# Dummy products of a recurrent-attention and maxout kernel in float32 instead of half precision, with new orders of work

## The chip, the cores and the metric

The kernel runs on one core of one Trainium2 chip. The metric is the device time in microseconds (us). In the profile PE is TensorE, DVE is VectorE, ACT is ScalarE, POOL is GpSimd and SP is SyncE, which here only issues loads. Stores are issued from ACT.

## The reference

The first part is a gated linear recurrence over 768 steps for 4 x 8 heads of width 48. Its output, as 3072 rows of 384, goes through a maxout layer with two weight matrices of 384 x 1024 and an output matrix of 1024 x 384. All data are float32.

```python
for t in range(S):
    state = alpha[:, :, t, :, None] * state + np.einsum('bhd,bhe->bhde', k[:, :, t], v[:, :, t])
    y[:, :, t] = np.einsum('bhd,bhde->bhe', q[:, :, t], state)
...
h1 = x @ w1
h2 = x @ w2
g = np.maximum(h1, h2)
return (g @ w_out).astype(np.float32)
```

## The kernel before, in words

The work is cut into 12 units of 256 time steps of one batch (u = 0 to 11), each of two chunks of 128 steps; units 0 and 1 are cut in two halves of four heads more. For a unit u the kernel loads alpha, k, q and v (`ld.af`, `ld.kf`, `ld.qf`, `ld.vf`, L345), takes the logarithm of alpha on ACT (`lg`), adds pairs of steps (`sg`, DVE or POOL, L459), and sums along time with a triangular matrix on PE (`cs`, L479 and L481). Exponentials of these sums (`em`, `ep`, `de` on ACT) scale k and q (`kn`, `qn`). PE transposes both (`tpk`, `tpq`, L507), multiplies them (`pp`, L533), and DVE masks the products (`pt`, L550 for the halves, L545 for whole units). `kv` (L582) makes a chunk's contribution to the state, `tm` and `sb` carry the state on, and `y` (L642) gives the recurrence's output, which `xt` takes to SBUF.

The maxout uses max(h1, h2) = h2 + relu(h1 - h2): `w12` is w1 - w2, the `h` steps (L672) multiply by it, `g` applies the relu (L677, L678), and the `o` steps (L699) multiply by w_out and add x times (w2 w_out). That last matrix is made in the kernel's head: w2 is transposed on PE in float32 (`wt`, L382), copied (`wtc`), and multiplied by w_out in half precision (`wq`, L404).

The order of everything is written by hand, or rather found by a search outside the kernel: `ORDERS` lists for PE, ACT, DVE, POOL and SP the steps in the order in which each engine runs them, and by being in an engine's list a step is also assigned to it. `Plan.follow` walks these lists with a duration for each step and a set of rules and gives every step a planned start and a PSUM bank. Among the rules is one for PE's instructions: it counts them (`ni` for each step, two for each product: a weight load and the product) and supposes that a new block of instructions must have arrived after 189 and then after every 256.

Where the plan shows PE without work for more than 0.25 us in the first 45 us, `gaps` and `fill` put dummy products on a scratch tile of zeros, `wsrc` (L819; the tile is cleared at L825 by the first DVE instruction, ahead of everything). A gap is filled up to 0.25 us before the planned start of the next step. In the gap that starts at the very beginning a product is reckoned at double time (`slow`). The dummies stand in PE's instruction stream between the real steps, and PE runs its stream in order. `Plan.fills` says how many dummies the plan counts for a gap.

Of the kernel before, what the change touches and what calls it, by code (L numbers as in the profile page):

```python
# [201 lines left out]
cs4 h2.3 h2.0 h2.2 pp3 cs5 h2.1 o2.1.x0 o2.0.x0 o2.0.f0 o2.1.f0 tpq4 tpk4 y3 o2.1.f1 o2.0.f1 o2.0.f2 o2.1.f2
o2.0.f3 pp4 o2.1.f3 h3.3 h3.1 h3.0 o3.0.x0 kv4 tpq5 tpk5 kv5 cs6 h3.2 o3.0.f0 o3.0.f1 o3.1.x0 y4 o3.1.f0 o3.1.f1
o3.0.f2 o3.1.f2 o3.1.f3 pp5 h4.2 cs7 h4.1 o3.0.f3 h4.0 tpk6 kv6 tpq6 y5 o4.0.x0 o4.1.x0 o4.1.f0 h4.3 h5.0
o4.0.f0 h5.1 o4.1.f1 o4.0.f1 o4.1.f2 o4.1.f3 tpq7 tpk7 pp6 o4.0.f2 o5.1.x0 cs8 o4.0.f3 h5.2 h5.3 o5.1.f0 o5.1.f1
y6 kv7 tpk8 tpq8 o5.1.f2 o5.0.x0 o5.1.f3 o5.0.f0 o5.0.f1 pp7 o5.0.f2 cs9 h6.3 o5.0.f3 h6.0 h6.2 y7 pp8 tpk9 tpq9
# [10 lines left out]
de1.0 qk0.0.0 ep0.1 qk0.0.1 vc1 w1.00 w0.11 qk1.0.0 qk1.1.0 qk1.1.1 woc.0 wtc.20 qk0.1.1 w0.01 w0.10 wtc.21
w1.10 wtc.10 wtc.00 woc.2 xt1.0 woc.3 wtc.01 woc.4 xt0.1 woc.5 g0.0 lg2 woc.6 g1.1 lg3 ra2 de2 em2 wqc.0 wqc.2
ep2 g1.2 ra3 g0.3 wqc.1 de3 em3 ep3 qk2.0 oc0.1 w2.01 w2.10 w2.11 oc1.1 vc3 oc0.0 lg4 lg5 xt2.0 ra4 oc1.0 em4
w3.00 ep4 de4 g2.0 g2.2 w3.11 w3.10 de5 ra5 lg6 em5 ep5 ra6 xt3.1 xt3.0 vc4 w4.01 oc2.0 vc5 oc2.1 g3.3 g3.1 g3.0  # L220
w4.00 st0 w5.01 qk5.0 de6 w4.10 em6 g3.2 ep6 lg7 xt4.0 xt4.1 lg8 oc3.1 g4.2 em7 g4.1 oc3.0 st1 ra7 w7.10 de7
w6.01 w6.00 xt5.1 xt5.0 ep7 lg9 g4.3 g5.0 ra8 g5.1 oc4.1 w6.11 qk7.0 em8 de8 st2 ep8 g5.2 g5.3 lg10 oc4.0 xt6.1
qk8.0 ra9 oc5.1 xt6.0 em9 g6.3 ep9 oc5.0 de9 g6.0 g6.2 w9.10 st3 xt7.0 vc8 qk9.1 g6.1 st4 g7.3 lg11 st5 vc10
g7.0 w9.11 ra10 em11 de11 ep11 w10.01 ra11 w10.11 em10 xt8.0 xt8.1 de10 ep10 oc7.0 xt9.1 g8.1 w11.00 xt9.0
w10.00 g8.2 st6 w11.11 st7 qk10.0 qk11.0 g9.0 g9.1 g9.2 g9.3 xt10.0 xt11.0 g11.2 st9 g10.2 oc8.0 g10.3 oc8.1 st8
oc10.0 oc10.1 st10 st11.0 oc11.1 st11.1 st11.2
# [3 lines left out]
q00.0 qn0.0 kn1.1 q01.1 dm0 q01.0 k01.0 k00.1 qn1.1 qn1.0 qn0.1 pt0.0.1 qk1.0.1 pt0.0.0 tm1.0 pt1.0.0 qk0.1.0  # L230
tm0.0 pt1.1.1 pt1.1.0 pt1.0.1 pt0.1.1 pt0.1.0 tm0.1 xt1.1 zw2 xt0.0 w12.0 tm1.1 w12.1 wtc.11 g1.0 w12.2 g0.2
g0.1 w12.3 sg3 q02 qn2 k02 kn2 dm3 g1.3 qk2.1 qn3 k03 w2.00 tm2.0 pt2.0 pt2.1 tm3.0 qk3.1 xt2.1 qk3.0 tm3.1 g2.3
tm2.1 qn4 pt3.1 pt3.0 g2.1 qk4.0 qk4.1 k05 sg6 pt4.0 qn5 pt4.1 tm4.0 qk5.1 tm5.0 tm4.1 sb5.1 w5.00 k06 tm5.1 qn6
sg7 dm6 pt5.0 pt5.1 tm6.0 g4.0 dm7 vc7 k07 qk6.0 qk6.1 qn7 sb6.1 w7.11 tm6.1 qk7.1 pt6.1 pt6.0 qn8 kn8 w7.01
tm7.0 qk8.1 k09 pt7.1 pt7.0 tm7.1 qn9 xt7.1 dm9 pt8.1 pt8.0 qk9.0 g7.2 g7.1 sg11 tm8.0 tm9.0 sb9.1 pt9.0 pt9.1
q011 k010 oc6.1 oc6.0 q010 w9.01 kn10 k011 w11.01 qn10 qn11 oc7.1 sb11.0 g8.0 tm11.0 qk11.1 g8.3 qk10.1 tm10.0
w11.10 pt10.0 pt10.1 sb10.1 w10.10 pt11.0 pt11.1 xt10.1 oc9.0 g10.0 xt11.1 g10.1 g11.1 oc9.1 g11.0 g11.3 oc11.0
oc11.2
# [509 lines left out]
def kernel(  # L748
# [63 lines left out]
    def fill(t0, t1, b):  # L812

        left = t1 - t0 - 0.25
        w = env["wsrc"]
        slow = 2.0 if t0 < 1.5 else 1.0
        while left > 0.06:
            cols = min(512, int(2400 * left / slow) - 5)
            nc.tensor.matmul(env["PB"][b][:, 0:cols], lhsT=w[:, 0:128], rhs=w[:, 0:cols], start=True, stop=True)  # L819
# [38 lines left out]
```

## Time and profile before

| | |
|---|---|
| median of three runs | 133.82 us (133.79 to 133.96) |
| the profiled execution's own time | 133.79 us |
| its span, first to last instruction | 132.1 us |
| PE busy | 124.8 us, 2061 products |
| DVE / ACT / POOL busy | 103.3 / 95.4 / 64.4 us |
| dummy products (L819) | 28, first at 1.3, last at 12.5 us |
| HBM read / written | 23.59 / 4.72 MB |

The rows of the timeline give a start and a length in us, the engine, the line, what is written and what is read, and how many instructions are merged; in brackets stands how long the engine was idle before and what ended that. PE's products overlap in a pipeline, so that the length of a row is longer than the distance to the next one. The rows by stage give for each stretch its length, then the busy time of PE, of PE's weight loads, of DVE, ACT and POOL, each with a count, then PE's granted clock, the share of the transfer engines and GB/s.

### The profile page before, as it was taken

The page shows a single profiled execution, that of the slowest core. Times are in us where ns is not written, and L with a number is a line of the kernel's source. Part 1 is how long each engine was busy: PE and PEld are TensorE (multiplying, and loading weights), DVE is VectorE, ACT ScalarE, POOL GpSimd, SP SyncE. Part 2 cuts the span into 40 slices and gives each one's busy share as a digit, 9 for nine tenths or more (in the row PEclk, how much of TensorE's full clock was granted, in tenths as well). Part 3 has the DMA queues.
Part 4 walks back from the last instruction along what each step waited for, and adds up shares of the span by engine and source line. Part 5 has one row for each costly group of instructions (what it writes and reads, how often), then busy time and mean ns, then how long its engine had stood idle before and what let it go on. Part 6 is the DMA issues. An engine that isn't in the chain of part 4 may idle for free.

```text
span 132.1 us, 4911 instructions
## 1 busy us (share of the span) xinstructions
PE 124.8 (95%) x2061; PEld 88.9 (67%) x2061; DVE 103.3 (78%) x186; ACT 95.4 (72%) x198; POOL 64.4 (49%) x104
## 2 busy tenths in 40 slices
PE   6988889999999999999999999999999999999970
PEld 2444667777667766867776767976688765778650
DVE  5469997869999996998699969989988599355040
ACT  3688889568899999998996997998288920301540
POOL 6025970052759999958579399655146200000000
PEclk9999999999999999999999999999999999999999
DMA  3999999999999999999999999560003300002144
GB/s 89 325 325 363 415 371 342 341 297 260 252 302 311 280 261 293 322 334 251 318 314 270 300 275 285 193 241 5 0 5 122 121 0 0 5 0 90 69 181 144
DMA packets 56486, 28.63 MB, mean 217 GB/s; under 512 B 50320, under 2 KB 56080, under 8 KB 56464
## 3 DMA queue, kind: packets, MB, share of 16 engines
...
q10 hardware_dynamic: 3424, 4.72, 9.9%
q8 instruction: 16, 0.26, 0.7%
q14 instruction: 6, 0.05, 0.1%
HBM read 23.59 MB, written 4.72 MB: 214 GB/s over the span
## 4 chain that ended last, share of the span: by engine, by line
PE 68%; SPq 7%; DVE 7%; DMA 6%; issue 4%; POOL 4%; DVEq 0%; POOLq 0%
PE pb L699 28%; PE pb L672 20%; PE pb L642 7%; SPq L345 6%; DMA w2f<-in_moe_w_dram 6%; PE pb L533 4%; PE pb L582 3%; PE pb L507 3%; PE pb L404 2%; SPq L367 2%; POOL kn L414 1%; DVE gt L677 1%; PE pb L382 1%; PE pb L479 1%; DVE w L417 1%
## 5 line engine op out<-in xcount | busy, mean ns | idle before, releaser
L699 PE MATMUL pb<-wo,gt 128*128 128x384 f16 (+2 forms) x200 | 37.5, 320 | 0.0
L672 PE MATMUL pb<-xt,w 128*128 128x256 f16 x288 | 36.5, 273 | 0.0
L672 PEld LDWEIGHTS <-w 128*128 128x128 f16 x288 | 27.6, 98 | 5.7
L678 ACT ACTIVATE gt<-pb 128x512 f16<-128x512 f32 x32 | 18.4, 600 | 11.5 <-PE pb L672 11.0
L545 DVE TENSOR_TENSOR pt<-pb,mask 128x1024 f16<-128x1024 f32 x20 | 23.6, 1217 | 2.5 <-PE pb L533 2.5
L699 PEld LDWEIGHTS <-gt 128*128 128x128 f16 x200 | 18.2, 98 | 9.9
L677 DVE TENSOR_SCALAR gt<-pb 128x512 f16<-128x512 f32 x16 | 10.9, 685 | 9.2 <-PE pb L672 8.8
L699 PE MATMUL pb<-w2o,xt 128*128 128x384 f16 (+2 forms) x75 | 15.2, 320 | 0.0
L417 ACT CAST xt<-pb 128x384 f16<-128x384 f32 x18 | 10.1, 592 | 5.6 <-PE pb L642 5.6
L414 POOL TENSOR_TENSOR sb<-tm,dd 128x384 f16<-128x384 f32 x15 | 12.9, 858 | 1.2 <-DVE tm L614 1.0
L614 DVE TENSOR_TENSOR tm<-pb,sb 128x384 f32<-128x384 f32 x16 | 8.6, 550 | 3.8 <-PE pb L582 3.5
L417 ACT COPY qk<-pb 128x1024 f16<-128x1024 f16 (+1 forms) x13 | 10.3, 818 | 1.6 <-PE pb L507 1.4
L417 ACT COPY os<-pb 128x384 f32<-128x384 f32 (+1 forms) x18 | 8.5, 473 | 3.9 <-PE pb L699 2.8
L819 PE MATMUL pb<-wsrc 128*128 128x512 f16 (+6 forms) x28 | 9.4, 480 | 1.3 <-DVE wsrc L825 1.3
L642 PE MATMUL pb<-pt,w 128*32 128x128 f16 x384 | 10.0, 220 | 0.0
L414 POOL TENSOR_TENSOR kn<-kf,em 128x768 f16<-128x768 f32 (+1 forms) x5 | 7.5, 1498 | 5.0 <-DVE kf L414 3.3
L417 DVE COPY qk<-pb 128x1024 f16<-128x1024 f16 (+1 forms) x15 | 9.5, 646 | 0.3
L414 POOL TENSOR_TENSOR qf<-qf,ra 128x384 f32<-128x384 f32 (+1 forms) x5 | 5.2, 1045 | 8.8 <-ACT pb L486 5.6
L484 ACT ACTIVATE em<-pb 128x384 f32<-128x384 f32 (+1 forms) x14 | 6.2, 442 | 4.5 <-PE pb L481 3.6
L642 PE MATMUL pb<-qk,sb 128*32 128x128 f16 x240 | 9.4, 219 | 0.0
L642 PEld LDWEIGHTS <-w 128*32 128x32 f16 x384 | 8.4, 96 | 1.5 <-issue 0.7
L699 PEld LDWEIGHTS <-xt 128*128 128x128 f16 x75 | 6.7, 98 | 3.5
(103 smaller groups left out, 232.1 us busy)
## 6 DMA issues: line engine op xcount, KB each, us to landing
...
```

The source lines that it names most:

```text
L345: nc.sync.dma_start(out=V(T_)[n].rearrange("p h r d -> p h (r d)"), in_=V(src)[b, :, t0 : t0 + 256, :].rearrange("h (p r) d -> p h (r d)", ...
L414: return lambda: getattr(nc, e).tensor_mul(out=o(), in0=x(), in1=y())
L417: return lambda: nc.scalar.copy(out=o(), in_=i()) if e == "scalar" else getattr(nc, e).tensor_copy(out=o(), in_=i())
L484: add(f"em{nq}", "ACT", lambda p=p, h_=h_: nc.scalar.activation(out=V("EM")[lg][:, h_], in_=csv(p), func=ACTF.Exp, scale=-1.0), 0.05 + 0.3 ...
L545: f = lambda e=e: nc.vector.tensor_mul(out=V("PT")[pt][:, e].rearrange("p a j x -> p (a j) x"), in0=pair(pp[e][0]).rearrange("p n (j x) -> ...
L614: nc.vector.tensor_add(out=V("TM")[new], in0=kvv, in1=V("SB")[m4])
L642: nc.tensor.matmul(o, lhsT=l, rhs=r, start=(a, qd) not in seen, stop=i == len(todo[qd]) - 1, skip_group_check=True)
L672: nc.tensor.matmul(t[:, m, :], lhsT=V("w12")[:, ds, f * 128 : f * 128 + 128], rhs=V("XT")[x3][:, ds, :], start=(ds == 0), stop=(ds == ND - 1))
L677: gd = lambda g2=g2, v2=v2: nc.vector.tensor_relu(out=g2(), in_=v2())
L678: ga = lambda g2=g2, v2=v2: nc.scalar.activation(out=g2(), in_=v2(), func=ACTF.Relu)
L699: nc.tensor.matmul(b32(x, w), lhsT=l, rhs=r, start=fst and y_ == 0, stop=lst and y_ == len(ws) - 1)
L819: nc.tensor.matmul(env["PB"][b][:, 0:cols], lhsT=w[:, 0:128], rhs=w[:, 0:cols], start=True, stop=True)
```

## The change

The scratch tile becomes float32, and with it both operands of every dummy product. The columns of a dummy are reckoned at 1200 per us instead of 2400, so that a 512-column dummy is reckoned at 0.43 us instead of 0.215 us at the full clock. The plan's count of a gap's instructions is halved with it, and for the gap at the very beginning halved again, which it had not been before.

```diff
-                    count += 2 * self.fills(t - pe - 0.25)
+                    count += 2 * self.fills((t - pe - 0.25) / (2 if pe == 1.2 else 1))
...
-        return int(left / 0.215) + (left % 0.215 > 0.06)
+        return int(left / 0.43) + (left % 0.43 > 0.06)
...
-    sbt("wsrc", [128, 512], FP16)
+    sbt("wsrc", [128, 512], FP32)
...
-            cols = min(512, int(2400 * left / slow) - 5)
+            cols = min(512, int(1200 * left / slow) - 5)
             nc.tensor.matmul(env["PB"][b][:, 0:cols], lhsT=w[:, 0:128], rhs=w[:, 0:cols], start=True, stop=True)
-            left -= (cols / 2400 + 0.002) * slow
+            left -= (cols / 1200 + 0.002) * slow
```

All five lists of `ORDERS` are new. The same 285 PE steps and the same loads are in them, and some steps change between ACT, DVE and POOL. The head of PE's list and of SP's list, before and after:

```diff
     "PE": """
-cs0.0 cs1.1 cs1.0 tpk0.0 cs0.1 tpq0.0 tpk1.1 pp0.0 tpk1.0 tpq1.1 kv1 tpq1.0 wt.20 pp1.0 tpq0.1 tpk0.1 kv0 pp1.1
-wt.21 pp0.1 wt.10 wq.20 wq.21 wt.00 wt.01 y1.0 y1.1 y0.0 y0.1 wq.00 wq.22 wq.01 wq.10 wq.02 wq.23 wq.03 wq.11
...
+cs1.0 cs1.1 cs0.1 cs0.0 tpk0.1 tpk0.0 tpq0.0 tpq0.1 pp0.0 pp0.1 tpk1.1 tpq1.1 wt.11 tpk1.0 pp1.1 tpq1.0 kv0 kv1
+pp1.0 wt.20 wt.00 wt.21 wt.10 y0.0 y0.1 y1.0 y1.1 wq.20 wq.21 wt.01 h0.0 wq.00 wq.10 wq.11 wq.22 wq.01 wq.12
...
     "SP": """
-ld.af0 ld.af1 ld.kf0 ld.kf1 ld.qf0 ld.qf1 ld.vf1 ld.vf0 ld.w2.2 ld.wo.0 ld.w2.1 ld.w2.0 ld.wo.1 ld.wo.2 ld.w1.0
+ld.af1 ld.af0 ld.kf0 ld.qf0 ld.qf1 ld.kf1 ld.vf0 ld.vf1 ld.w2.1 ld.w2.2 ld.w2.0 ld.wo.0 ld.w1.0 ld.wo.1 ld.w1.1
```

Further on, the part of PE's list in which the output products of units 8 and 9 stand:

```diff
-o6.1.f0 o6.1.f1 o7.1.f2 o6.1.f2 o6.1.f3 o6.0.f3 o7.0.x0 o7.0.f0 o7.0.f1 cs10 y8 y9 o7.0.f2 o7.0.f3 h8.3 h8.1
-o7.1.f3 h8.2 h8.0 tpq11 kv11 tpk10 tpq10 tpk11 o9.1.x0 h9.0 h9.1 o9.0.x0 h9.2 kv10 pp10 o9.1.f0 o9.0.f0 h9.3
+y9 y8 kv11 tpq11 tpk11 kv10 tpk10 tpq10 o9.0.x0 h8.0 h9.0 h8.3 h9.2 h8.1 h8.2 pp10 h9.1 o9.1.x0 o9.1.f0 o9.0.f0
```

More of the change, by code (lines that the diff above doesn't have):

```diff
@@ L202 @@
[L202 to L206, printed above, removed]
@@ L212 @@
-h10.2 o11.0.f0 o10.0.f1 o11.0.f1 o8.1.f3 o10.1.f1 o10.1.f2 o10.0.f2 h11.3 o10.0.f3 o11.1.f0 o11.0.f2 o10.1.f3
-o11.0.f3 o11.1.f1 o11.1.f2 o11.1.f3 o11.2.x0 o11.2.f0 o11.2.f1 o11.2.f2 o11.2.f3
+cs1.0 cs1.1 cs0.1 cs0.0 tpk0.1 tpk0.0 tpq0.0 tpq0.1 pp0.0 pp0.1 tpk1.1 tpq1.1 wt.11 tpk1.0 pp1.1 tpq1.0 kv0 kv1
+pp1.0 wt.20 wt.00 wt.21 wt.10 y0.0 y0.1 y1.0 y1.1 wq.20 wq.21 wt.01 h0.0 wq.00 wq.10 wq.11 wq.22 wq.01 wq.12
+wq.02 o0.0.f0 wq.13 wq.03 o0.1.f0 wq.23 h0.1 h1.0 wq.04 wq.14 wq.05 h1.2 wq.15 wq.24 wq.25 o1.1.f0 h0.2 h1.1
@@ new lines @@
+wq.16 wq.06 wq.26 wq.27 wq.17 cs2 o0.0.f1 o1.1.f1 wq.07 o0.1.f1 h0.3 cs3 o0.1.f2 o1.1.f2 h1.3 o0.0.f2 o0.1.f3
+o0.0.f3 tpq2 tpk2 o1.1.f3 o1.1.x0 o0.0.x0 kv2 pp2 o0.1.x0 o1.0.f0 o1.0.f1 o1.0.f2 o1.0.f3 tpq3 kv3 tpk3 y2
+o1.0.x0 cs4 h2.2 h2.0 pp3 o2.1.x0 h2.3 o2.1.f0 h2.1 cs5 o2.0.x0 o2.0.f0 o2.1.f1 o2.1.f2 y3 tpq4 tpk4 o2.0.f1
+o2.1.f3 o2.0.f2 o2.0.f3 cs6 h3.0 pp4 h3.1 h3.3 o3.1.x0 o3.1.f0 kv5 kv4 tpk5 tpq5 o3.1.f1 h3.2 o3.0.x0 o3.0.f0
+o3.0.f1 y4 pp5 o3.0.f2 o3.1.f2 h4.0 o3.0.f3 h4.3 o3.1.f3 tpq6 kv6 tpk6 y5 h4.1 cs8 o4.0.x0 h4.2 o4.0.f0 cs7
@@ new lines @@
+o4.0.f1 h5.0 h5.1 o4.0.f2 o4.0.f3 o4.1.x0 o4.1.f0 pp6 tpk7 tpq7 o4.1.f1 o4.1.f2 o4.1.f3 h5.2 h5.3 o5.1.x0 y6
+tpk8 kv7 tpq8 o5.1.f0 o5.1.f1 o5.0.x0 o5.0.f0 cs9 pp7 o5.1.f2 o5.1.f3 o5.0.f1 h6.2 o5.0.f2 o5.0.f3 h6.0 h6.3 y7
+tpk9 tpq9 pp8 h6.1 h7.3 h7.0 h7.2 h7.1 cs10 kv8 kv9 pp9 o6.1.x0 o6.0.x0 o6.0.f0 o6.1.f0 cs11 o6.0.f1 o7.1.x0
+o6.0.f2 o6.1.f1 o6.0.f3 o7.1.f0 o6.1.f2 o6.1.f3 o7.1.f1 o7.0.x0 o7.0.f0 o7.1.f2 o7.1.f3 o7.0.f1 o7.0.f2 o7.0.f3
+y9 y8 kv11 tpq11 tpk11 kv10 tpk10 tpq10 o9.0.x0 h8.0 h9.0 h8.3 h9.2 h8.1 h8.2 pp10 h9.1 o9.1.x0 o9.1.f0 o9.0.f0
@@ L214 @@
+o9.1.f1 o8.0.x0 h9.3 o8.0.f0 o9.0.f1 pp11 o9.0.f2 o8.0.f1 o8.1.x0 o8.1.f0 o9.0.f3 o8.1.f1 o8.1.f2 o9.1.f2 y10
+y11 o9.1.f3 o8.0.f2 o10.1.x0 o11.1.x0 o8.0.f3 h10.1 o8.1.f3 h10.0 o10.0.x0 h11.1 o10.0.f0 o10.1.f0 o10.1.f1
+h10.2 h10.3 h11.2 h11.0 o10.0.f1 o10.1.f2 o10.1.f3 o10.0.f2 o10.0.f3 o11.1.f0 h11.3 o11.0.x0 o11.0.f0 o11.0.f1
+o11.0.f2 o11.0.f3 o11.1.f1 o11.1.f2 o11.1.f3 o11.2.x0 o11.2.f0 o11.2.f1 o11.2.f2 o11.2.f3
 """,
     "ACT": """
-lg0.1 lg0.0 lg1.1 lg1.0 ra1.1 de0.0 ra0.0 em0.0 em1.0 ra0.1 em1.1 ep0.0 de0.1 ep1.1 ra1.0 em0.1 de1.1 ep1.0
@@ L217 @@
[L217 to L226, printed above, removed]
+lg1.1 lg1.0 lg0.1 lg0.0 ra0.1 em1.1 em1.0 ra1.0 em0.1 de1.1 ra0.0 de1.0 de0.0 ra1.1 ep0.1 ep1.1 em0.0 ep1.0
@@ new lines @@
+de0.1 ep0.0 qk0.1.0 qk0.1.1 w0.11 w1.11 vc1 qk1.1.1 w1.00 wtc.11 w0.01 qk1.0.0 w0.10 w1.01 wtc.20 woc.1 wtc.00
+wtc.21 xt0.1 xt0.0 wtc.10 g0.0 woc.4 lg2 ra2 lg3 ra3 g1.1 de2 wqc.1 em2 ep2 wqc.0 g0.3 em3 de3 wqc.2 ep3 g1.3
+vc2 oc1.1 oc0.0 w2.00 w2.01 vc3 oc0.1 lg4 w3.11 w3.10 xt2.0 ra4 em4 de4 oc1.0 lg5 g2.0 ra5 ep4 vc4 g2.1 de5 em5
+lg6 g2.3 ep5 xt3.1 ra6 w4.10 oc2.1 w4.00 de6 st0 vc5 g3.0 em6 g3.1 g3.3 ep6 w4.11 w5.00 w5.01 w5.10 g3.2 qk5.0
+lg7 xt4.1 w5.11 oc3.0 st1 ra7 lg8 w6.11 w6.00 xt5.1 g4.1 ra8 em8 g4.2 de8 ep8 de7 em7 g5.0 ep7 g5.1 oc4.0 w6.10
@@ L227 @@
+qk7.1 lg9 vc7 g5.2 st2 g5.3 xt6.0 qk8.0 ra9 em9 de9 vc8 w7.11 st4 ep9 lg11 w7.00 st3 oc5.0 g6.0 g6.2 lg10 xt7.0
+w9.11 st5 vc9 g6.1 ra10 ra11 g7.2 g7.3 g7.1 em10 em11 ep10 de11 de10 oc6.0 vc11 oc6.1 vc10 w9.10 w10.00 w8.10
+ep11 xt9.0 oc7.0 xt9.1 qk11.0 w11.00 qk10.0 qk10.1 g8.0 st6 g9.2 g8.1 g8.2 w11.10 g9.1 xt10.0 oc9.0 st7 xt11.1
+g10.1 g10.0 g10.2 st9 st8 g11.0 st10 g11.3 oc11.0 st11.0 oc11.1 st11.1 st11.2
 """,
     "DVE": """
-zw1 zqn0 ind zkn1 zqn2 zsb2 zsg1 zkn2 zqn1 zsg0 trj sg0.0 zsb0 own sg1.1 sg0.1 sg1.0 zw0 k00.0 zkn0 kn0.0 k01.1
@@ L230 @@
[L230 to L238, printed above, removed]
+zsg0 zw0 ind zkn0 trj own zsg1 zqn1 sg1.0 zsb3 zw1 zkn1 sg0.1 k00.1 zsb1 sg0.0 k00.0 kn0.1 zqn0 q00.1 q00.0 dm1
+kn0.0 q01.1 zqn2 qn0.0 qn0.1 k01.1 qk0.0.0 qk0.0.1 qn1.1 pt0.0.1 qn1.0 qk1.1.0 pt0.1.1 pt0.0.0 pt0.1.0 pt1.1.1
@@ new lines @@
+qk1.0.1 tm0.0 tm1.0 pt1.1.0 pt1.0.1 pt1.0.0 w12.0 xt1.0 tm1.1 wtc.01 xt1.1 w12.1 w12.2 tm0.1 woc.5 g1.0 g0.1
+g1.2 sg2 zw2 woc.6 g0.2 zkn2 sg3 w12.3 dm2 q02 qn2 kn2 q03 qn3 qk2.0 qk2.1 k03 tm2.0 pt2.1 pt2.0 tm3.0 tm2.1
+xt2.1 qk3.1 qk3.0 tm3.1 g2.2 pt3.0 sg5 pt3.1 qn4 q05 w4.01 xt3.0 qk4.0 qk4.1 qn5 oc2.0 pt4.0 pt4.1 tm5.0 tm4.0
+qk5.1 qn6 tm4.1 tm5.1 k06 xt4.0 pt5.1 pt5.0 g4.0 g4.3 qk6.0 sg8 sg7 xt5.0 k07 tm6.0 qk6.1 sb6.1 dm7 oc3.1 qn8
+qn7 k08 tm6.1 pt6.0 pt6.1 w8.01 qk7.0 xt6.1 tm7.0 oc4.1 qk8.1 sb7.1 tm7.1 pt7.1 pt7.0 oc5.1 qn9 g6.3 xt7.1 qk9.0
@@ L239 @@
+qk9.1 pt8.1 pt8.0 g7.0 sb9.0 tm9.0 tm8.0 pt9.0 pt9.1 sb9.1 k011 dm10 dm11 kn11 w9.00 qn10 qn11 xt8.0 xt8.1 oc7.1
+qk11.1 tm11.0 g8.3 tm10.0 g9.0 pt10.1 pt10.0 g9.3 sb10.1 pt11.1 pt11.0 xt10.1 xt11.0 g11.1 oc8.1 oc8.0 oc9.1
+g10.3 oc10.1 g11.2 oc10.0 oc11.2
 """,
     "POOL": """
-id16 id32 mask tri q00.1 kn1.0 dm1 dd0.1 vc0 w0.00 kn0.1 dd1.1 zsb3 woc.1 zsb1 sb1.1 w1.01 sb0.1 w1.11 woc.7 sg2
-dm2 dd2.1 q03 dd3.1 vc2 kn3 sb2.1 w3.01 sg4 sb3.1 sg5 q04 k04 dm4 kn4 q05 dd4.1 dm5 dd4.0 w4.11 dd5.0 sb4.0 kn5
@@ L243 @@
-q06 sb5.0 w5.10 dd5.1 sb4.1 w5.11 kn6 sg8 dd6.0 vc6 sb6.0 q07 kn7 dd6.1 dd7.0 q08 k08 dd7.1 w6.10 sb7.0 sg9 sg10
-dm8 sb7.1 dd8.0 q09 w7.00 sb8.0 kn9 w8.01 dd9.0 dd9.1 sb9.0 dd8.1 vc9 w8.11 w8.00 w8.10 vc11 dm11 dd11.1 sb8.1
-w9.00 kn11 dm10 dd11.0 dd10.0 sb10.0 sb11.1 dd10.1
+tri id16 mask sg1.1 dm0 id32 dd0.1 kn1.1 q01.0 k01.0 zsb2 kn1.0 vc0 zsb0 w1.10 w0.00 dd1.1 sb0.1 sb1.1 woc.0
+woc.2 woc.3 woc.7 k02 dm3 dd2.1 w2.11 w2.10 kn3 sb2.1 dd3.1 sg4 sb3.1 w3.01 q04 w3.00 dm4 k04 kn4 dm5 sg6 dd5.0
@@ L246 @@
+dd5.1 sb5.0 dd4.1 dd4.0 k05 dm6 kn5 sb4.0 q06 sb4.1 sb5.1 kn6 vc6 dd6.1 w6.01 q07 dd6.0 sb6.0 q08 kn7 dd7.1 kn8
+w7.10 dd7.0 sb7.0 dm8 k09 sg9 q09 dd8.1 w7.01 dm9 dd8.0 w8.11 kn9 sg11 w9.01 dd9.0 k010 sg10 w8.00 sb8.0 sb8.1
+dd9.1 q010 kn10 dd11.0 q011 w11.01 w10.10 w11.11 dd10.1 sb11.0 dd10.0 w10.11 dd11.1 w10.01 sb10.0 sb11.1
 """,
     "SP": """
-ld.af0 ld.af1 ld.kf0 ld.kf1 ld.qf0 ld.qf1 ld.vf1 ld.vf0 ld.w2.2 ld.wo.0 ld.w2.1 ld.w2.0 ld.wo.1 ld.wo.2 ld.w1.0
-ld.w1.1 ld.w1.2 ld.af2 ld.wo.3 ld.af3 ld.w1.3 ld.qf2 ld.kf2 ld.qf3 ld.vf2 ld.kf3 ld.vf3 ld.af4 ld.af5 ld.qf4
@@ L250 @@
-ld.kf4 ld.af6 ld.qf5 ld.vf4 ld.kf5 ld.vf5 ld.qf6 ld.kf6 ld.af8 ld.qf7 ld.af7 ld.vf6 ld.vf7 ld.af9 ld.kf7 ld.qf8
-ld.kf8 ld.kf9 ld.af10 ld.qf9 ld.vf8 ld.af11 ld.vf11 ld.vf9 ld.kf11 ld.vf10 ld.qf11 ld.kf10 ld.qf10
+ld.af1 ld.af0 ld.kf0 ld.qf0 ld.qf1 ld.kf1 ld.vf0 ld.vf1 ld.w2.1 ld.w2.2 ld.w2.0 ld.wo.0 ld.w1.0 ld.wo.1 ld.w1.1
+ld.w1.2 ld.wo.2 ld.af2 ld.af3 ld.wo.3 ld.w1.3 ld.qf2 ld.kf2 ld.qf3 ld.vf2 ld.kf3 ld.vf3 ld.af4 ld.af5 ld.qf4
+ld.kf4 ld.vf4 ld.af6 ld.qf5 ld.kf5 ld.vf5 ld.af7 ld.qf6 ld.kf6 ld.qf7 ld.vf6 ld.af8 ld.qf8 ld.kf7 ld.vf7 ld.kf8
@@ L252 @@
+ld.vf8 ld.af9 ld.kf9 ld.af10 ld.qf9 ld.af11 ld.vf9 ld.kf10 ld.vf11 ld.kf11 ld.qf10 ld.vf10 ld.qf11
 """,
```

6 lines of the change are left out of this document (removed).

## The prediction

> **What bounds the kernel now.** I read the page first (busy shares, chain by engine), then PE's waits, then busy time by stage, then PE's timeline of the first 14 us.
>
> ```profile
> PE 124.8 (95%) x2061; PEld 88.9 (67%) x2061; DVE 103.3 (78%) x186; ACT 95.4 (72%) x198; POOL 64.4 (49%) x104
> PE 68%; SPq 7%; DVE 7%; DMA 6%; issue 4%; POOL 4%; DVEq 0%; POOLq 0%
> PE pb L819 <- DVE wsrc L825: 1.3, 1, 1.3
> PE pb L382 <- DMA w2f<-in_moe_w_dram: 0.8, 2, 0.4
> PE pb L507 <- DVE qn L414: 0.6, 1, 0.6
> PE pb L507 <- DVE kn L414: 0.2, 1, 0.2
> ```
>
> PE is busy 95% of the span and heads the chain. All that it waits is four entries, 2.9 us, and the table by stage shows that they lie ahead of 19 us:
>
> ```profile
> 6.00:13.00 7.00, 6.18 (x79) 3.07 (x78) 5.88 (x19) 6.00 (x22) 2.13 (x5) 1.00 1.16 339
> 13.00:19.00 6.00, 5.01 (x103) 3.49 (x95) 5.88 (x12) 5.58 (x12) 5.79 (x11) 1.00 1.04 400
> 28.00:60.00 32.00, 31.92 (x569) 22.56 (x566) 29.73 (x45) 29.63 (x63) 24.25 (x31) 1.00 1.06 287
> 60.00:100.00 40.00, 39.93 (x766) 30.06 (x765) 35.83 (x53) 33.20 (x68) 25.83 (x41) 1.00 0.70 200
> 100.00:128.00 28.00, 28.00 (x404) 20.76 (x402) 16.13 (x25) 11.03 (x21) 2.30 (x4) 1.00 0.16 59
> ```
>
> From 28 to 128 us PE is busy 99.85 of 100 us (first busy column). There is no slack there: whatever is late when the dense stage begins is late at the end, and a better order can win back little in it. The head decides. Most of PE's time there is dummy work, L819:
>
> ```profile
> 1.25 4.85 PE L819 MATMUL pb<-wsrc 128*128 128x512 f16 x11 [1.25 <-DVE wsrc L825]
> 5.89 0.37 PE L479 MATMUL pb<-sg,tri 128*128 128x192 f16 x1
> 6.15 0.88 PE L819 MATMUL pb<-wsrc 128*128 128x512 f16 x2
> 6.83 0.36 PE L479 MATMUL pb<-sg,tri 128*128 128x192 f16 x1
> 7.09 0.24 PE L479 MATMUL pb<-sg,tri 128*128 128x192 f16 x1
> 7.22 0.97 PE L819 MATMUL pb<-wsrc 128*128 128x512 f16 x4
> 8.12 0.29 PE L507 MATMUL pb<-ident,kn 64*128 64x64 f16 x8
> 8.49 1.01 PE L819 MATMUL pb<-wsrc 128*128 128x512 f16 x4
> 10.15 0.29 PE L507 MATMUL pb<-ident,qn 64*128 64x64 f16 x8 [0.65 <-DVE qn L414]
> 10.84 1.20 PE L819 MATMUL pb<-wsrc 128*128 128x512 f16 x5
> 11.97 0.40 PE L533 MATMUL pb<-qk 48*128 48x128 f16 x8
> 12.30 0.46 PE L819 MATMUL pb<-wsrc 128*128 128x512 f16 x2
> 12.70 0.30 PE L507 MATMUL pb<-ident,kn 64*128 64x64 f16 x8
> ```
>
> ```profile
> L819 PE MATMUL pb<-wsrc x28: 233/390/634, 1.3 to 12.5; 128*128 128x512 f16 x22, 128*128 128x479 f16 x1, 128*128 128x354 f16 x1, 128*128 128x388 f16 x1
> ```
>
> Two things are to be seen. The dummies are in PE's own order, so a real product that stands behind them waits until they are through: the first scan product (L479) starts at 5.89, where the eleven dummies end. And PE's clock rises near 7.09 us: the same 192-column product takes 0.37 and 0.36 before and 0.24 after. Eleven dummies took (5.89 - 1.25) / 11 = 0.42 us each at the slow clock.
>
> **The cost of a float32 column.** No float32 product is in the trace, but float32 transposes are (L382), and they give the first bound:
>
> ```profile
> L382 PEld LDWEIGHTS pb<-ident,w2f x24: 138/140/144, 14.1 to 23.2; 128*128 128x128 f32 x24
> L382 PE MATMUL pb<-ident,w2f x24: 272/273/330, 14.1 to 23.3; 128*128 128x128 f32 x24
> 23.10 0.44 PE pb L382 x4
> 26.63 1.98 PE pb L672 x18
> ```
>
> Four transposes of 128 columns take 0.44 us of the chain, 0.11 each or 0.86 ns a column; eighteen half-precision products of 256 columns take 1.98, 0.11 each or 0.43 ns a column. So moving float32 data costs PE double. The change's arithmetic (columns / 1200 per us) is this figure: 512 columns for 0.44 us. It holds if a float32 product is one such pass. A transpose, however, only passes one operand through against ones and zeros; a product has a second float32 operand, in the weights, and if that too must be taken in two parts, the pass is run twice: 0.88 us for 512 columns. No row decides between them. Lower bound 0.44, upper bound 0.88 (an estimate: the doubling of the row applied to both operands). I take 0.88, since copying a value needs one pass where multiplying two wide numbers needs the partial products of both, and keep 0.44 as a rival.
>
> The Trainium skill, FP8 and Floating Point Precision, TensorE Precision Notes, states that a true float32 product takes four passes through the array (both halves of the one operand with both halves of the other). By it 512 columns would take four times 0.22 us, an estimate of 0.87 us, and the sum below stays; by the transposes' row alone it would be the first rival's 133.4. No run here shows which.
>
> **The first fill.** It spans 4.64 us at the slow clock. The new code reckons 0.857 us for a 512-column product there, so it issues 4.64 / 0.857 = 5.4 products. At two passes and the slow clock one costs 2 x 0.88 = 1.76 us. From 1.25 until the clock rises at 7.09 that is 3.3 products; the other 2.1 take 0.88 each, 1.85 us, and the first scan product starts at about 8.9 instead of 5.9: 3.0 us late. Were the clock to stay low, 5.4 x 1.76 would end at 10.8, 4.9 late. At one pass it would be late by nothing.
>
> **The later fills.** By their rows they hold PE for 0.68 (6.15 to 6.83), 0.90 (7.22 to 8.12), about 0.94 (1.01, less the 0.07 by which the row before runs into its successor), 1.13 and 0.40, together 4.05 us, of which I take five mode changes of 0.08 off: 3.65 us. Doubled, they add 3.65; the 0.25 us which the code leaves free in each gap takes up 5 x 0.25. Remainder 2.4 us. Together with the first fill PE is up to 5.4 late at 12.7 us.
>
> **What of it reaches the end.** Some is absorbed, by waits on transfers, which do not move:
>
> ```profile
> 7.91 0.36 DVE L414 TENSOR_TENSOR kf<-kf,af 128x192 f32<-128x192 f32 x1 [0.21 <-DMA kf<-in_k_dram]
> 9.05 0.36 DVE L414 TENSOR_TENSOR qf<-qf,ra 128x192 f32<-128x192 f32 x1 [0.78 <-DMA qf<-in_q_dram]
> 16.73 3.08 DVE L550 TENSOR_TENSOR pt<-pb,mask 128x512 f16<-128x512 f32 x5
> 11.11 7.76 DMA w2f<-in_moe_w_dram
> 19.00 1.06 PE pb L382 x8
> ```
>
> DVE waits 0.99 us for loads before it becomes dense; then it is busy 5.88 of the 6 us from 13 to 19, masking what PE's L533 products make, and those masked tiles are what the first output products need at 20 us. Thus lateness passes from PE through DVE to the dense stage. The least that arrives is the first fill's 3.0 less 0.99, 2.0 us; the most is 5.4 less the 0.78 us that PE waits for w2, 4.6 us. I take the middle, 3.3.
>
> **The new orders.** In PE's list the changes between the 128-row, 64-row and 32-column ways of using the array go from 55 to 49, of which from the first output product on from 46 to 44. Four dummies before 8.12 have 3 x 512 + 388 columns, 0.82 us at 0.43 ns; the next tiled group starts 0.90 after their start. So a change costs 0.08 us, and two save 0.16. w2's last block is loaded before the first of w_out instead of after one: with the two waits of 0.8 us this can save up to 0.8, but only if PE is on time; where PE is 3 us late those waits are gone already. The reassignments among ACT, DVE and POOL lie beside a full PE from 28 us on: I cost them at nothing, covered by PE's 99.85 busy us; if the cover fails somewhere, PE waits for a single step, up to 0.7 us (one pt row, 3.08 / 5 plus its start).
>
> The wider scratch tile is cleared by DVE ahead of everything:
>
> ```profile
> 0.92 0.27 DVE L825 MEMSET wsrc<- 128x256 uint32 x1 [0.92 <-PEq L842]
> 2.26 0.22 DVE L330 MEMSET sb<- 128x192 uint32 x1
> 3.68 0.09 DVE L293 MEMSET tri<- 64x32 uint32 x1 [0.77 <-POOL tri L288]
> ```
>
> 64 more words cost 0.05 us, so 256 more cost 0.2; PE's first dummy starts that much later. DVE's later clearing is hidden by its 0.77 us wait for the triangle; PE's shift isn't, and lies within the 3.3's spread.
>
> **Sum.** 133.79 us of the profiled execution (span 132.1, the rest around it; the median is 133.82) + 3.3 - 0.16 = 136.9 us.
>
> **Rivals.** *One pass* (the other side): the float32 product costs what the transposes cost. Then fills end where planned, the head keeps its time, the orders save 0.16 and about half of w2's 0.8, and the clearing costs 0.2: 133.79 - 0.16 - 0.4 + 0.2 = 133.4 (132.8 to 134.0). For it: the only float32 rows. Against: those are no products. It decides from a product of at most 0.44 us. Chance 0.20.
>
> *Absorbed*: products are double, but the new head starts its steps in an order in which transfers end last, and less than 0.5 us arrives: 134.0. For it: a transfer share above 1 from 6 to 19 us (last column but one of the stages). Against: DVE's full stretch. Chance 0.06.
>
> *Instruction supply*: products are double, and each is two pairs of instructions, so the stream isn't shorter by half; the plan's count is off by some 30.
>
> ```profile
> q8 instruction: 16, 0.26, 0.7%
> out_dram<-os ACTq DMA_DIRECT2D x1, 64.0 KB, 1.8
> 95.56 1.68 PE pb L642 x112
> ```
>
> Sixteen blocks serve 2 x 2061 PE instructions, one block for about 258. The new list puts y9 y8 kv11 tpq11 tpk11 kv10 tpk10 tpq10 together, 192 short products in some 3 us (112 of them in 1.68), over a block in 2.1 us. If a block comes late there, PE stalls; none of PE's four waits in the trace is of this kind, so the price is between 0 and the 1.8 us that the smallest store takes to land; half of that on top of the forecast gives 137.8. Chance 0.08. The Trainium skill, Runtime: NRT & Kernel Launch, Instruction fetch mechanics, holds that blocks of 256 instructions are streamed ahead and a crossing is mostly hidden; by this fewer instructions earn nothing, as PE's waits here bear out.
>
> **How the numbers follow.** Forecast 136.9, chance 0.66, its own range 135.5 to 139.0 (2.0 to 4.6, and the memset). The whole range takes in most of *one pass* below and a clock that rises late above: 133.2 to 139.4. About 0.2% (0.27 us) can be told from no change. Faster: three quarters of *one pass*, 0.15. Same: 0.07, from *one pass* and *absorbed*. Slower: 0.78.
>
> **What would show it.** Right: float32 dummies with twice as many MATMUL rows as products, about 30, each near 0.44 us apart at the full clock and 0.87 before; the first L479 at 8 to 10 us; PE's waits for w2 gone; the dense stage from 28 us as long as before but shifted. Wrong: some 15 dummy rows, the first L479 near 6 us.

## The result and the profile after

The changed kernel takes 137.69 us (137.24 to 137.89) against 133.82: slower, with a ratio of 1.0282, 95% interval [1.0256, 1.0309]. The profiled execution took 137.89 us with a span of 136.2. The forecast was 136.9. Ratios here leave out single executions that took over 1.5% longer than the shortest of their kernel.

The page of the changed kernel (busy time, the chain by engine, the group of the dummies, now L818 because the file is one line shorter):

```profile
PE 130.5 (96%) x2073; PEld 93.5 (69%) x2073; DVE 104.2 (77%) x189; ACT 91.7 (67%) x188; POOL 68.9 (51%) x111
PE 91%; DVE 5%; issue 1%; DVEq 0%
L818 PE MATMUL pb<-wsrc 128*128 128x512 f32 (+10 forms) x40 | 17.5, 569 | 1.5 <-DVE wsrc L824 1.5
```

PE heads the chain for 91% of the span instead of 68%: the stretch in which the kernel waited for its loads is gone from the chain, and PE's own stream has taken its place. The profile has more dummy rows than before, not fewer: 40 instead of 28, and PE has 2073 rows instead of 2061.

The view of the dummies' tile (duration as least, median and most):

```profile
L818 PEld LDWEIGHTS pb<-wsrc x40: 186/190/338, 1.5 to 19.8; 128*128 128x128 f32 x40
L818 PE MATMUL pb<-wsrc x40: 213/592/1222, 1.5 to 20.2; 128*128 128x512 f32 x20, 128*128 128x57 f32 x2, 128*128 128x187 f32 x2, 128*128 128x95 f32 x2
L824 DVE MEMSET wsrc<- x1: 485/485/485, 1.0 to 1.0; 128x512 f32 x1
```

Every size that the row shows stands there an even number of times: the program asks for 20 products, and each is run as two passes with a weight load each. A weight load takes 190 ns where the half-precision one took 98, and the clearing takes 0.485 us where it took 0.272.

PE's timeline of the changed kernel, the dummies with the first scan product (L478) and the first output product (L641):

```profile
1.52 7.75 PE L818 MATMUL pb<-wsrc 128*128 128x512 f32 x12 [1.52 <-DVE wsrc L824]
9.11 0.25 PE L478 MATMUL pb<-sg,tri 128*128 128x192 f16 x1
9.38 0.56 PE L818 MATMUL pb<-wsrc 128*128 128x187 f32 x2
9.91 1.30 PE L818 MATMUL pb<-wsrc 128*128 128x512 f32 x4
11.18 1.02 PE L818 MATMUL pb<-wsrc 128*128 128x463 f32 x2
12.36 2.29 PE L818 MATMUL pb<-wsrc 128*128 128x512 f32 x6
14.92 0.48 PE L818 MATMUL pb<-wsrc 128*128 128x121 f32 x2
15.55 1.42 PE L818 MATMUL pb<-wsrc 128*128 128x512 f32 x4
17.23 0.45 PE L818 MATMUL pb<-wsrc 128*128 128x75 f32 x2
18.17 1.36 PE L818 MATMUL pb<-wsrc 128*128 128x512 f32 x4
19.80 0.97 PE L818 MATMUL pb<-wsrc 128*128 128x479 f32 x2
24.63 0.34 PE L641 MATMUL pb<-pt,w 128*32 128x128 f16 x10
```

The first scan product starts at 9.11 instead of 5.89, and none of the rows shown after the first has an idle time in brackets: ahead of 20 us PE waits for no other engine once its dummies have begun; it is always late. The first output product starts at 24.63; in the kernel before it was 19.99. From there on PE is as full as before, as the waits and the stages show (same columns as in the prediction):

```profile
PE pb L818 <- DVE wsrc L824: 1.5, 1, 1.5
PE pb L532 <- DVE qk L416: 0.4, 1, 0.4
13.00:19.00 6.00, 6.00 (x72) 3.61 (x71) 4.46 (x13) 3.31 (x8) 5.04 (x11) 1.00 1.04 393
28.00:60.00 32.00, 32.00 (x493) 22.88 (x492) 29.41 (x47) 26.45 (x57) 19.51 (x29) 1.00 1.01 273
60.00:100.00 40.00, 39.88 (x752) 29.77 (x745) 38.28 (x58) 33.40 (x66) 29.58 (x39) 1.00 0.78 219
100.00:128.00 28.00, 28.00 (x501) 21.24 (x499) 16.17 (x25) 13.74 (x24) 6.67 (x13) 1.00 0.14 49
```

PE's waits for w2 are gone. Its one wait behind the dummies, 0.4 us for `qk`, stands at 22.41, and from 1.52 us up to it the chain that ended last runs through PE's own stream; DVE has only the two steps just ahead of that wait:

```profile
21.35 0.68 DVE pt L549
22.02 0.34 DVE qk L416
```

From 28 to 128 us PE is busy 99.88 of 100 us. So the time can be read as a sum: the start of the first output product, the dense stage behind it up to the start of the last product, and the end. The next table gives these starts from the traces, one execution for each kernel, with the medians of the experiments told below.

| kernel | first scan product | first output product | last product | dense stage | median, us |
|---|---|---|---|---|---|
| before | 5.89 | 19.99 | 127.83 | 107.84 | 133.82 |
| changed | 9.11 | 24.63 | 132.34 | 107.71 | 137.69 |
| e1: new orders, float32 that fits | 6.04 | 19.18 | 127.60 | 108.42 | 132.56 |
| e2: new orders, half precision | 5.65 | 19.02 | 127.78 | 108.76 | 133.21 |
| e3: old orders, float32 as in the change | 8.05 | 23.56 | 131.42 | 107.86 | 137.33 |
| e4: float32 in the first fill only | 8.25 | 21.05 | 128.75 | 107.70 | 134.44 |
| e5: float32 in the later fills only | 5.85 | 22.04 | 129.74 | 107.70 | 134.67 |
| e6: no dummies | 5.66 | 20.93 | 128.97 | 108.04 | 133.83 |
| e7: e2 with six dummies fewer | 5.58 | 19.45 | 127.37 | 107.92 | 133.18 |
| e8: old orders, float32 that fits | 5.86 | 21.30 | 129.07 | 107.77 | 134.07 |
| e9: e1 again | 5.78 | 19.08 | 127.50 | 108.42 | 132.79 |
| e10: e2 again | 5.49 | 19.40 | 127.11 | 107.71 | 133.32 |

### The profile page after: what moved, and what is told of

It reads as the page before. It is cut to its first block, busy times and chain, and to the rows that moved or that the text cites. A ratio compares the mean times of both kernels' runs of the same rounds, so it can differ in the third digit from the quotient of the medians.

```text
span 136.2 us, 4928 instructions
## 1 busy us (share of the span) xinstructions
PE 130.5 (96%) x2073; PEld 93.5 (69%) x2073; DVE 104.2 (77%) x189; ACT 91.7 (67%) x188; POOL 68.9 (51%) x111
## 4 chain that ended last, share of the span: by engine, by line
PE 91%; DVE 5%; issue 1%; DVEq 0%
PE pb L698 32%; PE pb L671 22%; PE pb L818 12%; PE pb L641 7%; PE pb L506 4%; PE pb L532 4%; PE pb L403 3%; PE pb L581 2%; PE pb L381 2%; DVE pt L544 2%; PE pb L478 2%; DVE qk L416 1%; DVE sg L458 1%; PE pb L480 1%; DVE gt L676 1%
## 5 line engine op out<-in xcount | busy, mean ns | idle before, releaser
L698 PE MATMUL pb<-wo,gt 128*128 128x384 f16 (+2 forms) x200 | 38.2, 320 | 0.0
L677 ACT ACTIVATE gt<-pb 128x512 f16<-128x512 f32 x33 | 19.2, 596 | 13.8 <-PE pb L671 11.1
L818 PE MATMUL pb<-wsrc 128*128 128x512 f32 (+10 forms) x40 | 17.5, 569 | 1.5 <-DVE wsrc L824 1.5
L676 DVE TENSOR_SCALAR gt<-pb 128x512 f16<-128x512 f32 x15 | 10.0, 686 | 7.4 <-PE pb L671 7.3
L818 PEld LDWEIGHTS pb<-wsrc 128*128 128x128 f32 x40 | 7.9, 218 | 8.5 <-issue 6.7
L413 POOL TENSOR_TENSOR kn<-kf,em 128x768 f16<-128x768 f32 (+1 forms) x7 | 11.1, 1582 | 4.9 <-PE pb L581 2.0
L416 ACT CAST xt<-pb 128x384 f16<-128x384 f32 x12 | 7.0, 598 | 7.0 <-PE pb L641 7.0
L416 ACT COPY qk<-pb 128x1024 f16<-128x1024 f16 (+1 forms) x10 | 8.2, 838 | 5.0 <-PE pb L506 4.3
L416 DVE COPY qk<-pb 128x1024 f16<-128x1024 f16 (+1 forms) x18 | 10.8, 624 | 0.8 <-PE pb L506 0.6
L641 PE MATMUL pb<-pt,w 128*32 128x128 f16 x384 | 10.0, 220 | 0.0
L641 PEld LDWEIGHTS <-w 128*32 128x32 f16 x384 | 8.4, 96 | 2.1 <-issue 1.8
L641 PE MATMUL pb<-qk,sb 128*32 128x128 f16 x240 | 9.4, 219 | 0.0
L416 ACT COPY os<-pb 128x384 f32<-128x384 f32 (+1 forms) x14 | 6.6, 470 | 3.7 <-PE pb L698 3.7
```

The lines of the kernel that those rows point to most:

```text
L413: return lambda: getattr(nc, e).tensor_mul(out=o(), in0=x(), in1=y())
L416: return lambda: nc.scalar.copy(out=o(), in_=i()) if e == "scalar" else getattr(nc, e).tensor_copy(out=o(), in_=i())
L641: nc.tensor.matmul(o, lhsT=l, rhs=r, start=(a, qd) not in seen, stop=i == len(todo[qd]) - 1, skip_group_check=True)
L676: gd = lambda g2=g2, v2=v2: nc.vector.tensor_relu(out=g2(), in_=v2())
L677: ga = lambda g2=g2, v2=v2: nc.scalar.activation(out=g2(), in_=v2(), func=ACTF.Relu)
L698: nc.tensor.matmul(b32(x, w), lhsT=l, rhs=r, start=fst and y_ == 0, stop=lst and y_ == len(ws) - 1)
```

## The experiments

The theory: a float32 dummy takes two passes of 0.43 us per 512 columns, double what the code reckons, and the overrun reaches the dense stage (the prediction had it pass through DVE). The rivals: it is the new orders that are slower; or the number of instructions, which is not what the plan counts, makes PE stall.

**e1, the dummies reckoned at what they take.**

```diff
-            cols = min(512, int(1200 * left / slow) - 5)
+            cols = min(512, int(600 * left / slow) - 5)
...
-            left -= (cols / 1200 + 0.002) * slow
+            left -= (cols / 600 + 0.004) * slow
```

> The changed kernel, but a float32 dummy is reckoned at 600 columns per us, so that half as many products fill a gap; orders and plan stay. Theory (a float32 product is run as two passes of 0.43 us per 512 columns, and the overrun is passed on): the first scan product starts at about 6.2 us, the first output product at 20 us, 22 or fewer dummy rows, and the time falls to what the new orders alone give, 133.0 to 134.2 us. Rival (the new orders are what is slower): 136.5 us or more, although the dummies fit. Rival (instruction supply): the stream is now as short as the plan counts, so it would gain beyond e2 by 0.5 us or more.

Measured: 132.56 us (132.49 to 133.12), ratio to the kernel before 0.9862 [0.9789, 0.9935], below the range; there are 26 dummy rows, where 22 or fewer were expected. PE's timeline of e1 and its waits ahead of the first output product:

```profile
1.52 4.73 PE L818 MATMUL pb<-wsrc 128*128 128x512 f32 x6 [1.52 <-DVE wsrc L824]
6.04 0.37 PE L478 MATMUL pb<-sg,tri 128*128 128x192 f16 x1
19.18 0.34 PE L641 MATMUL pb<-pt,w 128*32 128x128 f16 x10
PE pb L506 <- DVE qn L413: 0.5, 1, 0.5
PE pb L532 <- DVE qk L416: 0.3, 1, 0.3
```

With two lines changed the first output product starts 5.45 us earlier than in the changed kernel, and the time falls by 5.1. The new orders are not what is slower: with dummies that fit they beat the kernel before. With these orders the overrun is the whole loss. The dense stage is 0.7 us longer here than in the changed kernel, because PE now comes early enough to be held up near 51 and 52 us, where 0.40 and 0.30 us pass from one product's start to the next; the first wait stands in this row:

```profile
51.02 0.81 PE L671 MATMUL pb<-xt,w 128*128 128x256 f16 x6 [0.24 <-DVE qk L416]
```

**e2, new orders with the dummies of before.**

```diff
-    sbt("wsrc", [128, 512], FP32)
+    sbt("wsrc", [128, 512], FP16)
...
-            cols = min(512, int(1200 * left / slow) - 5)
+            cols = min(512, int(2400 * left / slow) - 5)
...
-            left -= (cols / 1200 + 0.002) * slow
+            left -= (cols / 2400 + 0.002) * slow
```

> The changed kernel with the dummies of before: half-precision tile, 2400 columns per us; orders and plan stay, so PE's stream has some 30 to 60 instructions more than the plan counts. Theory (overrun of the float32 dummies): 133.0 to 134.2 us, within 0.3 us of e1. Rival (new orders are slower): 136.5 or more. Rival (instruction supply): slower than e1 by 0.5 us or more, with PE idle ahead of a step without a releaser.

Measured: 133.21 us (133.05 to 133.64), 0.9934 [0.9902, 0.9965]. That is within the theory's range, but 0.65 above e1, as the rival of instruction supply has it, and the trace shows its stall. The waits, the timeline and the stage that ends in the stall, with the count of PE's products in its first bracket:

```profile
PE pb L641 <- issue: 0.8, 1, 0.8
19.44 0.26 PE L641 MATMUL pb<-pt,w 128*32 128x128 f16 x4
20.55 0.24 PE L641 MATMUL pb<-pt,w 128*32 128x128 f16 x4 [0.84 <-issue]
0.00:19.60 19.60, 16.40 (x222) 9.41 (x222) 15.14 (x53) 14.33 (x37) 11.28 (x30) 1.00 0.98 311
```

In the middle of the first output products, which need nothing more from any engine, PE stands for 0.84 us without a releaser. It has run 222 products and 222 weight loads, together 444 instructions, and the plan's rule has a new block begin after 189 + 256 = 445. In the trace's records of transfers the block for this place started at 17.93 and had landed at 19.10, and PE went on at 20.55. The dense stage of e2 is longer than the shortest by 108.76 - 107.70 = 1.06 us, the whole step from one product to the next at this place (19.48 to 20.55).

**e3, the dummies' change alone on the old orders.** The edit is that of the change's tile and `fill`, on the kernel before; its plan and orders stay.

> The kernel before with its orders and plan, but float32 dummies reckoned at 1200 columns per us as in the change. Theory: the dummies alone cost 3 to 5 us: first scan product at about 9 us, 137 to 139 us. Rival (new orders are slower): 134.0 us, with the lateness taken up before 20 us.

Measured: 137.33 us (137.19 to 137.96), 1.0228 [1.016, 1.0295], within the theory's range, but with the first scan product at 8.05 instead of about 9. The first output product moves from 19.99 to 23.56, by 3.57 us, and the time by 3.4. PE's timeline of e3:

```profile
8.05 0.25 PE L479 MATMUL pb<-sg,tri 128*128 128x192 f16 x1
23.56 0.24 PE L642 MATMUL pb<-pt,w 128*32 128x128 f16 x4
```

So float32 dummies are slower without the new orders too, by 1.9 us less at the first output product. About half of that is there already at the first scan product, which is 2.16 us late here (8.05 against 5.89) and 3.07 in the changed kernel (9.11 against 6.04 in e1), though the first fill has twelve rows from 1.52 us on in both. The starts of these rows show why: 512-column rows begin 0.853 us apart until 5.0 us in e3 and until 7.65 in the changed kernel, and 0.43 apart after that. PE's clock rose 2.65 us earlier in this execution of e3. The later fills overrun by the same in both: they hold PE for 7.50 us against 4.05 in the kernel before, and for 8.96 in the changed kernel against 5.51 in e1. The other half fits the waits that lateness can use up before the first output product. PE has 1.6 us of them in the kernel before and none left in e3, against 0.8 in e1 and 0.4 left in the changed kernel.

**e4 and e5, the overrun in the first fill only and in the later fills only.** Both read the same cleared tile, in half precision where the other rate applies (e5 has the condition the other way round).

```diff
-            cols = min(512, int(1200 * left / slow) - 5)
+            rate = 1200 if t0 < 1.5 else 2400
+            v = w if rate == 1200 else w.bitcast(FP16)
+            cols = min(512, int(rate * left / slow) - 5)
-            nc.tensor.matmul(env["PB"][b][:, 0:cols], lhsT=w[:, 0:128], rhs=w[:, 0:cols], start=True, stop=True)
-            left -= (cols / 1200 + 0.002) * slow
+            nc.tensor.matmul(env["PB"][b][:, 0:cols], lhsT=v[:, 0:128], rhs=v[:, 0:cols], start=True, stop=True)
+            left -= (cols / rate + 0.002) * slow
```

> The changed kernel, float32 dummies (1200 columns per us) in the first fill only; the later fills read the same zeros as half precision at 2400 columns per us. Theory, by the prediction's terms: the first scan product at 9.1 us as in the changed kernel; of its 3.0 us lateness 2.0 to 2.5 reach the end: 135.4 to 136.2. Rival (the first fill is hidden behind the loads of q and k, the later fills cost all): 133.5 to 134.2.

> The changed kernel with half-precision dummies (2400 columns per us) in the first fill and float32 ones (1200 columns per us) in the later fills, the counterpart of e4. First output product: 24.6 us in the changed kernel, 21.1 in e4, 19.2 in e1, so the first fill is worth 1.9 us of lateness and the later fills should be worth 3.5: first output product at about 22.6 and 135.5 to 136.5 us. Rival (the lateness of both together is what counts, because the later fills alone are absorbed by the waits for q and w2): 133.0 to 134.2.

Measured: e4 134.44 us (133.56 to 135.16), 1.0018 [0.9977, 1.0059]; e5 134.67 (134.34 to 135.43), 1.0046 [1.0013, 1.0079]. Both lie between the theory's range and the rival's. The first output product starts at 21.05 and 22.04, that is 1.87 and 2.86 us later than in e1; both overruns together give 5.45, 0.7 more than the two added. The first fill is the same in e4 and in the changed kernel, but the first scan product starts at 8.25 in e4, not at the 9.1 that was expected. The e4 rows beside those of the changed kernel above:

```profile
1.52 6.90 PE L820 MATMUL pb<-wsrc 128*128 128x512 f32 x12 [1.52 <-DVE wsrc L826]
8.25 0.25 PE L478 MATMUL pb<-sg,tri 128*128 128x192 f16 x1
```

The same twelve rows are through 0.86 us earlier, because in e4's execution their distance falls from 0.85 to 0.43 us at 5.94 instead of 7.65. So the 0.7 us by which the two overruns seem to add to more than their sum need no link between them: the moment at which the clock rises differs by more. The rest of the difference from the expected times is e1's: each lateness is paid less by the 0.7 us which PE waits in e1's dense stage and no longer waits when it is late (107.70 in both). That e4's times spread over 1.6 us fits a clock that rises at different moments; with one trace of e4 it is not shown.

**e6, no dummies.**

```diff
-P.gaps(45.0, 0.25)]
+P.gaps(0.0, 0.25)]
```

> The changed kernel with no dummy products at all; orders and plan stay. It tells what the dummies are for. If they only raise PE's clock early: the clock rises late, the 192-column scan products keep 0.37 us, products up to the first output products take double, and the end is 1 to 4 us later than e1: 133.6 to 136.6. Rival (the head is bound by loads and DVE, and PE's clock there costs nothing): 132.3 to 133.2.

Measured: 133.83 us (133.36 to 134.51), 0.9992 [0.9962, 1.0022]: at the low end of what was expected and as long as the kernel before, some 1.0 to 1.3 above e9 and e1, and 0.5 to 0.6 above e10 and e2, which have the same orders and half-precision dummies. What the dummies buy is seen in sixteen transposes, the first row of e6, the second of e1:

```profile
17.82 3.18 PE L381 MATMUL pb<-ident,w2f 128*128 128x128 f32 x16
```

```profile
17.29 1.97 PE L381 MATMUL pb<-ident,w2f 128*128 128x128 f32 x16
```

They take 1.2 us longer where no dummy has kept PE going, and the first output product starts at 20.93 instead of 19.18. The trace's record of the granted clock begins only at 20.36 us in e6; in e1 it begins at 6.68. So the whole filling is worth between half a microsecond and 1.3, and doing it with an overrun costs five. e6 also shows the other stall without a releaser (waits, timeline, and the stage up to it):

```profile
PE pb L641 <- issue: 0.4, 1, 0.4
64.88 0.22 PE L641 MATMUL pb<-qk,sb 128*32 128x128 f16 x1
65.52 0.23 PE L641 MATMUL pb<-qk,sb 128*32 128x128 f16 x1 [0.42 <-issue]
0.00:65.00 65.00, 55.48 (x990) 41.86 (x990) 56.46 (x117) 50.63 (x110) 39.70 (x70) 1.00 1.03 295
```

It comes after 990 products and as many weight loads, 1980 instructions, and 189 + 7 x 256 = 1981. Its block had landed at 64.10 by the records of transfers. In both stalls PE goes on 1.4 us after the landing (20.55 - 19.10, 65.52 - 64.10).

**e7, e2 with six dummies fewer.** The last dummy of each later fill is left out where the fill has two or more.

```diff
-            nc.tensor.matmul(env["PB"][b][:, 0:cols], lhsT=w[:, 0:128], rhs=w[:, 0:cols], start=True, stop=True)
-            left -= (cols / 2400 + 0.002) * slow
+            rest = left - (cols / 2400 + 0.002) * slow
+            if rest > 0.06 or t0 < 1.5 or left == t1 - t0 - 0.25:
+                nc.tensor.matmul(env["PB"][b][:, 0:cols], lhsT=w[:, 0:128], rhs=w[:, 0:cols], start=True, stop=True)
+            left = rest
```

> e2 (new orders, half-precision dummies) with the last dummy of each later fill left out where the fill has two or more, six pairs of instructions fewer, so that PE's stream is as long as in e1. Theory (instruction supply: in e2 PE stood 0.8 us in the middle of the first output products, without a releaser, where a block of instructions landed at 19.1 us after waiting from 12.7): with twelve instructions fewer ahead of it the boundary falls on another product and is reached later, the stall goes and the time is e1's, 132.3 to 132.8. Rival (e1's gain over e2 is something else, such as the later start of the dummies or chance): 133.0 to 133.4, the stall still there.

Measured: 133.18 us (132.89 to 133.94), 0.9933 [0.9905, 0.9961]. The stall is not in the trace (of an execution of 132.89 us, the shortest), but the time is e2's. Here PE waits ahead of the first output products instead:

```profile
18.02 1.50 PE L381 MATMUL pb<-ident,w2f 128*128 128x128 f32 x12 [0.51 <-DVE pt L549]
19.45 0.34 PE L641 MATMUL pb<-pt,w 128*32 128x128 f16 x10
```

So the expectation failed in its time: twelve instructions fewer did not give e1's. Whether they are what removed the stall is not shown; e10 below has none either, with e2's own instructions.

**e8, float32 that fits, on the old orders.** The kernel before with the tile of the change and e1's two lines.

> The kernel before with its orders and plan, and float32 dummies reckoned at 600 columns per us, so that they fit. Theory (the overrun is all of what float32 costs): 133.6 to 134.2 us, as before, first scan product at about 6.1 us. Rival (float32 dummies cost something beside the overrun, such as the longer clearing or the weight loads): 134.5 or more. If e8 is at 133.9 and e1 at 132.6, the new orders are worth 1.3 us.

Measured: 134.07 us (133.17 to 135.75), 0.9986 [0.9941, 1.003]. That is as expected: nothing clear of noise is left of e3's loss, so the overrun was all that float32 cost on these orders, to within the interval's 0.4 us. The times spread over 2.6 us. In the profiled execution, one of the long ones (135.03 us), PE waits for w2; whether the others differ by the same is not shown.

```profile
16.12 0.63 PE L382 MATMUL pb<-ident,w2f 128*128 128x128 f32 x4 [1.34 <-DMA w2f<-in_moe_w_dram]
```

**e9 and e10, e1 and e2 again in more rounds, on the same chip.**

> The kernel of e1 (new orders, float32 dummies reckoned at 600 columns per us), timed beside that of e2 in more rounds. From the traces so far the time is the start of the first output product plus 107.7 us of full PE, plus what PE stalls after it, plus the end. If the shorter stream is worth its 0.7 us (no stall between the first output products): 132.4 to 132.7, and 0.5 or more below e10. If e1 had only met early transfers: 132.9 to 133.3, as e10.

> The kernel of e2 (new orders, half-precision dummies) beside e9. 133.0 to 133.4 in both cases; in its trace PE stalls again among the first output products for 0.5 us or more if the block of instructions lands after it is wanted.

Measured: e9 132.79 us (132.47 to 134.33), 0.9929 [0.9899, 0.9959]; e10 133.32 (132.62 to 133.88), 0.9942 [0.9915, 0.997]. Both beat the kernel before again; e9 lies between the two times that were expected for it, and e10 within its own. The medians are 0.53 us apart in e9's favour, after 0.65 between e1 and e2, and nine of e9's twelve executions took 133.02 us or less against four of e10's. The kernels differ, then, but the cause stays open: e10's profiled execution, the shortest of its twelve (132.62 us), has no stall among the output products. Its block had landed at 16.79 us, well before PE came to that place at 19.88; in e2 it landed at 19.10 and PE was there at 19.48. So the stall comes in one execution of this kernel and not in another. How many of the longer executions have it, and so whether the shorter stream is worth its half microsecond, no trace shows.

## Why the prediction was right, point by point

*The float32 column*: right. The upper bound of 0.88 us for 512 columns was taken; two passes of 0.43 were measured, shown by the 40 rows for 20 products (about 30 rows were forecast; the new plan has nine later fills instead of five). The rival of one pass is thereby out. The trace agrees in the price with the four passes of the Trainium skill (FP8 and Floating Point Precision, TensorE Precision Notes); as rows it shows two of double length.

*The first fill*: right in its mechanism. 8.9 was forecast for the first scan product, 9.11 measured; the dummies began 0.27 us later than before behind the longer clearing, which was forecast at 0.2. That the size was so close is partly luck: the forecast took 7.09 us for the rise of the clock, the changed kernel's execution had 7.65, and with 5.94 in e4 the same fill ended at 8.25.

*The later fills*: their doubling was taken from the fills of the old orders, 3.65 us. The new orders' nine fills hold PE for 8.96 us against 5.51 in e1, where they fit: 3.45 more, as on the old orders (7.50 against 4.05). The term was good for both.

*What reaches the end*: this is the term that was mis-sized. It was 3.3, the middle between 2.0 and 4.6, so 2.1 of the 5.4 us were taken to be absorbed. On the old orders, from which it was worked out, e3 measured 3.57, with the help of a clock that rose at 5.0 us. On the new orders it is 5.45 (19.18 to 24.63), all of the 5.4 us by which PE was reckoned late: 3.07 up to the first scan product and 2.38 behind it, against 3.0 and 2.4. The waits that were to absorb some of it were those of the old head: e1 has no wait for w2 that lateness could use up. The path was another, too. The prediction had the lateness pass from PE through a DVE that is busy 5.88 of the 6 us from 13 to 19. In the changed kernel DVE is busy 4.46 of them and PE 6.00; the dummies hold up PE itself, and from 1.52 us to the first output product DVE has 1.02 us of the chain.

*The new orders*: forecast at 0.16 us, measured at 1.2 to 1.3 with float32 dummies that fit (e9 and e1 against their kernel before, 133.95 and 133.90) and at 0.6 to 0.7 with half-precision ones (e10 and e2). The part in the dense stage came out in size: 107.84 becomes 107.71, 0.13, though no run shows that it is the two mode changes. Missed was the head, where the first output product starts 0.8 us earlier; the prediction saw that w2 now comes ahead of w_out and took nothing for it in the sum, because PE would be late. That was a mistake in the account: the lateness is counted from where the new orders would have been. Missed as well was the end, from the start of the last product to the end of the span: it is 4.24 us in all three traces with the old orders (before, e3, e8) and 3.80 to 3.83 in all nine with the new ones, so the new orders save 0.4 us there. The errors, +2.1 for the lateness and -0.8 and -0.4 for the orders, partly cancel; that the sum missed the profiled time by only 1.0 us is partly luck.

*The rivals*: absorption is out; the lateness went into the dense stage, which takes 107.70 us in e4 and e5 and 107.71 in the changed kernel, and only the 0.7 us which PE waits in e1's dense stage is won back. Instruction supply did not act in the changed kernel, which has no such stall, but it is real in e2 and e6, at another place than the prediction named. The sentence drawn from the Trainium skill (Runtime: NRT & Kernel Launch, Instruction fetch mechanics), that crossings are mostly hidden, agrees with most of the sixteen blocks of each kernel; at two crossings the traces differ, by 0.84 us (e2) and 0.42 us (e6) of idle PE. And fewer instructions per filled microsecond is what float32 dummies do give once they fit: 26 rows in e1 against 32 in e2.
